# Attention of two tiles done together every second tile in a chunked-attention and SoLU feed-forward kernel

## The chip, the cores and the metric

The kernel runs on one core of a Trainium2 chip. The metric is the device time of one execution in microseconds (us), lower is better; three runs of the kernel before gave a median of 517.52 us. A core has TensorE (PE, matrix products into PSUM), VectorE (DVE), ScalarE (ACT), GpSimd (POOL) and SyncE (SP, which issues DMAs); each works through its own instructions in order and waits on semaphores for the others. DMAs are issued here by SyncE, GpSimd and ScalarE.

## The reference

Attention within chunks of 64 positions, for 8 batches of 8 heads with 576 positions and head size 64; its output, 4608 tokens of 512, goes through a feed-forward layer with the SoLU activation (h times its softmax) and a normalization:

```python
scores = scale * np.matmul(q_c, k_c.transpose(0, 1, 2, 4, 3))
attn = softmax of scores (with the maximum taken off, and 1e-09 added to the sum)
out = np.matmul(attn, v_c)
...
x = out, transposed and reshaped to (B * S, H * D)
h = x @ w_in
e = np.exp(h - h_max)
solu = h * e / (sum(e) + 1e-09)
ln = (solu - mu) / np.sqrt(var + 1e-06) * g_ln
return ln @ w_out
```

All inputs are fp32 (the weights arrive as fp64). The layer has 1024 hidden columns.

## The kernel before

**Tiles.** The 4608 tokens are 36 tiles of 128, two chunks of 64 each; a batch is 4.5 tiles. Tile i passes through attention (scores, softmax, values) and then the feed-forward layer. Every large product is made three times with operands split into a high and a low part (`x_h`, `x_l`, `wi_h`, `wi_l`, and so on).

**TensorE's work for a tile.** `scores(i)`: 32 products of 64 x 64, from `QT` and `KT`. `values(i)`: 32 more, from `V` and the transposed attention weights `AT` (in the profile `attn_t`). Both write the PSUM tile `sx` of two banks, scores in one half and values in the other. `ffn_in(i)`: 24 products of 128 x 512 into `ph` (two banks). `ffn_out`: 24 more into `po`, issued in three thirds by `third()`, for a tile three places behind. PSUM has eight banks: `ph` 2, `sx` 2, `tp` 2 (transposes at the start and end of the kernel), `po` 2.

**The way of the attention weights.** `softmax_a(i)` takes the row maximum of the scores (`s_nmax`) and the difference (`e`) on VectorE and the exponential on ScalarE; `softmax_b(i)` sums (`s_sum`), inverts and multiplies on VectorE. `attn_turn(i)` transposes 32 x 32 blocks into `a_b`; after an odd tile, eight DMAs of 64 KB, four of SyncE and four of GpSimd, put the blocks of two tiles into place in `AT`, of which there is one buffer for an even and an odd tile. `x_high` and `x_low` then split the values for `ffn_in`: `x_h` on ScalarE, `x_l` on VectorE.

**The SoLU.** `solu_a`: row maximum `h_nmax` (VectorE) and the exponential `z` with its sum (ScalarE). `solu_b`: product of `ph` and `z` with its sum (VectorE), `nmean` (VectorE, one column), and the mean taken off (ScalarE). `solu_c`: `ssum` and `eps`, one column each on VectorE. `variance`: squares `sq` with their sum (ScalarE), `u` (VectorE, one column), `r` = u to the power -0.5 (GpSimd, one column). `z_turn(i)` transposes blocks of `z` into `z_b`, and after an odd tile 16 DMAs carry them into `z_t`; `z_split` splits that into `z_h` and `z_l`, the operands of `ffn_out`; `store` scales the result by `r` into `o_sb` and stores it (256 KB, issued by ScalarE).

**Order.** Up to the loop, tiles and the conversion of the weights are interleaved by the list of words `START` (one word is one call: `K:7` is `qk_turn(7)`, `q:14` issues 14 loads, `C` converts weights, `F` is a third of `ffn_out`); there the framework's scheduler may reorder instructions. In the loop, from tile 5 on, `order.on` keeps the instructions of each engine in program order. `load_some(n)` issues n of the 32 loads of a batch of queries and keys on SyncE, 72 KB each; `qk_turn` transposes a tile's queries and keys from them on VectorE. Before, one iteration i does, in this order: `load_v` and `qk_turn` of i+3, `z_turn(i-1)`, `z_split`, loads, `ffn_in(i)`, `scores(i+3)`, `values(i+1)`, `solu_a(i)`, a third, `softmax_a(i+3)`, `x_high(i+1)`, `solu_b(i)`, `softmax_b` and `attn_turn` of i+3, loads, `x_low(i+1)`, `solu_c(i)`, a third, `variance(i)`, a third.

All calls of the loop go through the wrapper at line 42, so most rows of the profile show L42, and instructions are told apart by the names of their tiles.

Of the kernel before, what the change touches and what calls it, by code (L numbers as in the profile page):

```python
# [19 lines left out]
S:1 N:2 C:1 n:3 C:1 C:1 A:1 P:5 P:6 v:1 B:1 V:0 S:2 T:1 M:0 X:0 C:1 A:2 v:2 C:1 P:7 N:3  # L20
B:2 Y:0 C:1 V:1 Q:1 T:2 C:1 n:4 S:3 A:3 v:3 q:8 R:0 V:2 M:1 q:8 X:1 N:4 B:3 S:4 C:1 A:4
q:8 Y:1 M:2 z:0:0 q:8 K:5 X:2 Y:2 T:3 V:3 K:6 C:1 z:0:1 R:1 Q:2 S:5 B:4 T:4 A:5 S:6 v:4
V:4 B:5 T:5 v:5 F F A:6 K:7 C:1 B:6 C:1 R:2 M:3 v:6 Z:2 F z:1:0 X:3 Y:3 S:7 M:4 q:14 R:3
z:1:1 X:4 A:7 B:7 Y:4 V:5 U:6 F U:7 q:14 Z:3 R:4 v:7 F F
"""


# [23 lines left out]
def chunk_attention_then_solu_ffn(  # L51
# [10 lines left out]
    nc = tc.nc  # L62
# [9 lines left out]
    NCC = DM // P  # L72
    NFC = FF // P
    SCALE = 1.0 / float(D) ** 0.5
    LO_DVE = (0, 6, 7, 10, 14)
    LO_TT = (0, 1, 3, 5, 6, 8)
    LO_POOL = (0, 1, 3, 4, 5)
# [13 lines left out]
    small = ctx.enter_context(tc.tile_pool(name="small", bufs=3))  # L91
    ps_h = ctx.enter_context(tc.tile_pool(name="ps_h", bufs=1, space=PSUM))
    ps_a = ctx.enter_context(tc.tile_pool(name="ps_a", bufs=1, space=PSUM))
    ps_t = ctx.enter_context(tc.tile_pool(name="ps_t", bufs=2, space=PSUM))
    ps_o = ctx.enter_context(tc.tile_pool(name="ps_o", bufs=2, space=PSUM))

    order = Order(tc)
# [3 lines left out]
        for e in (nc.tensor, nc.vector, nc.scalar, nc.gpsimd, nc.sync)  # L101
    )

    ident = const.tile([P, P], F32, name="ident")
    make_identity(nc, ident)
    mhalf = const.tile([P, 1], F32, name="mhalf")
    nc.gpsimd.memset(mhalf, -0.5)
    g_sb = const.tile([P, NFC], F32, name="g_sb")
    ident_r = const.tile([P, P], F32R, name="ident_r")
    nc.vector.tensor_copy(out=ident_r, in_=ident)  # L110
# [237 lines left out]
    def turn_natural(i):  # L348
        qk_tiles(i)
        for x in range(2):  # L350
            t = nat[:, i % 2, x]
            pt = ps_t.tile([P, HP, P], F32, name="tp")
# [10 lines left out]


    sx = ps_a.tile([P, 2, 2, HP, CH], F32, name="sx")

    def scores(i):
        for hp in range(HP):
# [14 lines left out]
        MS.memset(ES[x][:, :, CH:], 1e-9)  # L383

    def softmax_a(i):
        sv = sx[:, :, 0].rearrange("p j a k -> p a j k")
# [12 lines left out]
        act.activation(e, e, AF.Exp, scale=SCALE)  # L399
        st[i, "e"] = e  # L400
# [17 lines left out]
    def attn_transpose(i):  # L418

        a = st.pop((i, "e"))  # L420
        pt = ps_t.tile([P, HP, P], F32, name="tp")
        for hp in range(HP):
            pe.transpose(
                pt[:, hp, :],
                a[:, 2 * hp:2 * hp + 2, :].rearrange("p j k -> p (j k)"),
                ident,
            )
        for c in range(2):
            cols = slice(c * CH, (c + 1) * CH)
            to = AT[cols, :, i % 2].rearrange("p g (h j) t -> p j h g t", j=2)  # L430
            for j in range(2):
                act.copy(
                    to[:, j],
                    pt[j * CH:(j + 1) * CH, :, cols].rearrange(
                        "p h (g t) -> p h g t", t=32
                    ),
                )
# [20 lines left out]
                        )  # L458

    def values(i):  # L460
        for hp in range(HP):
            for j in range(2):
                for c in range(2):
                    rows = slice(c * CH, (c + 1) * CH)
                    pe.matmul(
                        sx[j * D:(j + 1) * D, c, 1, hp],
                        V[i][rows, 2 * hp + j, :],
                        AT[rows, :, i % 2, 2 * hp + j, :],
                        start=True,
                        stop=True,  # L470
                    )
        if not order.on:
            x_high(i)
            x_low(i)

    def x_high(i):
        xv = sx[:, :, 1].rearrange("p c a t -> p a c t")
        xh = work.tile([P, NCC, P], F32R, name="x_h")
        xl = work.tile([P, NCC, P], F32R, name="x_l")
        xhv, xlv = (x.rearrange("p a (c t) -> p a c t", t=CH) for x in (xh, xl))  # L480
        act.copy(xhv, xv)
        st[i, "x"] = xh, xl

    def x_low(i):
        xv = sx[:, :, 1].rearrange("p c a t -> p a c t")
# [32 lines left out]
    def solu_b(i):  # L518
        ph = st.pop((i, "h")).rearrange("p n f -> p (n f)")
        z, esum = st.pop((i, "he"))  # L520
        zsum = small.tile([P, 1], F32, name="z_sum")
        dve.scalar_tensor_tensor(
            out=z, in0=ph, scalar=1.0, in1=z, op0=ALU.mult, op1=ALU.mult,
            accum_out=zsum,
        )
        nmean = small.tile([P, 1], F32, name="nmean")
        dve.tensor_scalar(
            out=nmean, in0=zsum, scalar1=-1.0 / FF, scalar2=None, op0=ALU.mult
        )
        if order.on:  # L530
            act.activation(z, z, AF.Identity, bias=nmean)
        else:
            pool.tensor_scalar(
                out=z, in0=z, scalar1=1.0, scalar2=nmean, op0=ALU.mult, op1=ALU.add
            )
        st[i, "z"] = z, esum
        if not order.on:
            solu_c(i)

    def solu_c(i):  # L540
        z, esum = st[i, "z"]

        ssum = small.tile([P, 1], F32, name="ssum")
        dve.tensor_scalar(
            out=ssum, in0=esum, scalar1=1e-9, scalar2=None, op0=ALU.add
        )
        eps = small.tile([P, 1], F32, name="eps")
        dve.scalar_tensor_tensor(
            out=eps, in0=ssum, scalar=1e-6, in1=ssum, op0=ALU.mult, op1=ALU.mult
        )  # L550
        st[i, "z"] = (z, eps)

    def variance(i):
        z, eps = st.pop((i, "z"))
        sq = work.tile([P, FF], mybir.dt.bfloat16, name="sq", bufs=1)
        ssq = small.tile([P, 1], F32, name="ssq")
        act.activation(sq, z, AF.Square, accum_out=ssq)
        u = small.tile([P, 1], F32, name="u")
        dve.scalar_tensor_tensor(
            out=u, in0=ssq, scalar=1.0 / FF, in1=eps, op0=ALU.mult, op1=ALU.add  # L560
        )
# [41 lines left out]
    def z_transpose(i, f):  # L603

        z, _ = st[i, "n"]
        pt = ps_t.tile([P, NFC // 2, P], F32, name="tp")
# [8 lines left out]
    def ffn_out(i, part, parts):  # L615
# [2 lines left out]
        halves = 2 if i == NT - 1 else 1  # L618
        if part == 0:
            st[i, "o"] = [  # L620
                (ps_o, ps_t)[x].tile([P, DM], F32, name=("po", "tp")[x])
                for x in range(halves)
            ]
        ops = []
# [36 lines left out]

    def load_g():
        nc.sync.dma_start(g_sb, g_ln.rearrange("(a p) -> p a", p=P))

    loads = []

# [54 lines left out]
    for i in range(first, NT):  # L721
        order.on = i >= ORD

        if i + 3 < NT and next_batch < B and chunk_of(i + 3, 0)[0] == next_batch - 1:
            load_batch(next_batch)
            next_batch += 1
        if i + 3 < NT:
            load_v(i + 3)
            qk_turn(i + 3)
        if not direct(i - 1):  # L730
            z_turn(i - 1)
        z_split(queue[0][0], slice(0, NFC))
        ahead = i == NT - 1
        load_some(4 if i % 2 == 0 else 6)
        ffn_in(i)

        if i + 3 < NT:
            scores(i + 3)
        if i + 1 < NT:
            values(i + 1)  # L740
        solu_a(i)

        def part():
# [5 lines left out]
        part()  # L749
        if i + 3 < NT:  # L750
            softmax_a(i + 3)
        if i + 1 < NT:
            x_high(i + 1)
        solu_b(i)
        if i + 3 < NT:
            softmax_b(i + 3)
            attn_turn(i + 3)
        load_some(3 if i % 2 == 0 else 5)
        if i + 1 < NT:
            x_low(i + 1)  # L760
        solu_c(i)
        part()
        variance(i)
        part()
# [34 lines left out]
```

## Time and profile before

| | |
|---|---|
| runs | 516.67, 517.52, 517.53 us (median 517.52) |
| profiled execution | 519.47 us, of which the span from first to last instruction is 517.7 us |
| mean granted clock of TensorE | 0.98 |
| busy: TensorE, VectorE, ScalarE, GpSimd | 94%, 79%, 52%, 33% of the span |
| chain that ended last | TensorE 82%, VectorE 8%, DMA 3%, ScalarE 2% |

In the profile's rows, L42 is the line of the kernel, `out<-in` names the tiles written and read, `xN` counts instructions, and a bracket shows how long the engine had been idle and what ended that. A row of TensorE that merges several products shows their first start and last end; the ends are modelled, and so starts are compared. "SPq" and "ACTq" are DMA issues of SyncE and ScalarE. "DMA to landing" is the time from the start of an issue to its arrival, for those whose arrival could be told. A row of stretches gives, after the length, the busy time of PE, PEld (weight loads), DVE, ACT and POOL, and then the granted clock of TensorE, the DMA engines' share and GB/s.

### The profile page before, as it was taken

Reading aid. Unit: us, or ns where it says so; the run is one execution under the profiler, and the core shown is the slowest. Engines: PE = TensorE matmul, PEld = TensorE weight load, DVE = VectorE, ACT = ScalarE, POOL = GpSimd, SP = SyncE. Lnnn points to the kernel's source line nnn. Section 1 sums busy time; section 2 is a strip of 40 time slices with the busy share of each in tenths; the row PEclk is TensorE's granted clock in tenths of the full one; section 3 lists DMA queues with packets and bytes.
Section 4 is the critical chain, followed back from the end, with each engine's and each line's share of the span. In section 5 each row is a group of like instructions: output and inputs, shape, how many; then the busy total and the mean of one; then the engine's idle time right before and its main releaser. Section 6 shows DMA issues by size and latency. Waiting matters only on the chain.

```text
span 517.7 us, 11241 instructions
## 1 busy us (share of the span) xinstructions
PE 485.9 (94%) x4190; PEld 388.7 (75%) x4190; DVE 408.5 (79%) x714; ACT 268.3 (52%) x412; POOL 170.2 (33%) x291
## 2 busy tenths in 40 slices
PE   3779879989999999999999999999899999999997
PEld 2355657768887888888888888888688888887876
DVE  5999976777888888888888888888678888874531
ACT  4858764534444455555555555454355554444452
POOL 4774742540413223131313131413231405043300
PEclk9988979989999999999999999999899999999999
DMA  9996794530777566767576448675747434352211
GB/s 272 347 234 149 127 161 75 126 103 22 170 148 172 133 152 140 169 163 152 145 160 153 108 125 163 158 167 147 141 128 157 120 106 126 80 144 73 79 47 48
DMA packets 204454, 72.33 MB, mean 140 GB/s; under 512 B 188592, under 2 KB 189104, under 8 KB 204016
## 3 DMA queue, kind: packets, MB, share of 16 engines
q1 hardware_dynamic: 192800, 49.58, 43.9%
q0 software_dynamic: 6272, 12.60, 9.4%
q10 hardware_dynamic: 5328, 9.44, 4.9%
q8 instruction: 33, 0.54, 0.4%
q14 instruction: 21, 0.17, 0.1%
HBM read 36.97 MB, written 9.44 MB: 90 GB/s over the span
## 4 chain that ended last, share of the span: by engine, by line
PE 82%; DVE 8%; DMA 3%; ACT 2%; issue 2%; SPq 1%; POOL 0%; ACTq 0%; DVEq 0%
PE po L42 39%; PE ph L42 35%; PE sx L42 7%; DVE w_a L42 4%; DMA attn_t<-a_b 2%; PE tp L42 1%; SPq L42 1%; DMA nat<-in_k_dram 1%; DVE w_p L42 1%; DVE h_nmax L42 1%; ACT z L42 1%; DVE z L42 0%; DMA q_st<-in_q_dram 0%; DVE s_sum L42 0%; ACT o_sb L42 0%
## 5 line engine op out<-in xcount | busy, mean ns | idle before, releaser
L42 PE MATMUL ph<-wi_l,x_h 128*128 128x512 f32 x288 | 114.8, 399 | 8.5 <-ACT w_r L42 3.6
L42 PE MATMUL po<-wo_l,z_h 128*128 128x512 f32 (+1 forms) x288 | 115.9, 402 | 0.3 <-ACT z_h L42 0.3
L42 PE MATMUL ph<-wi_h,x_h 128*128 128x512 f32 x288 | 114.4, 397 | 0.0
L42 PE MATMUL po<-wo_h,z_l 128*128 128x512 f32 (+1 forms) x288 | 112.4, 390 | 0.0
L42 PE MATMUL po<-wo_h,z_h 128*128 128x512 f32 (+1 forms) x288 | 112.3, 390 | 0.0
L42 ACT ACTIVATE z<-ph,h_nmax 128x1024 f32<-128x1024 f32 x36 | 40.2, 1116 | 138.6 <-DVE h_nmax L42 138.6
L42 DVE TENSOR_REDUCE h_nmax<-ph 128x1 f32<-128x1024 f32 x36 | 44.0, 1223 | 48.7 <-PE ph L42 48.6
L42 POOL DMA_DIRECT2D z_t<-z_b x136 | 67.6, 505 | 36.3 <-DVE z_b L42 32.0
L42 PE MATMUL ph<-wi_h,x_l 128*128 128x512 f32 x288 | 78.5, 391 | 0.7 <-DVE x_l L42 0.7
L42 POOL TENSOR_TENSOR r<-u,mhalf 128x1 f32<-128x1 f32 x36 | 20.5, 569 | 175.7 <-DVE u L42 165.1
L42 PEld LDWEIGHTS ph<-wi_l,x_h 128*128 128x128 f32 x288 | 55.3, 192 | 21.5 <-ACT wo_l L42 4.0
L42 PEld LDWEIGHTS po<-wo_l,z_h 128*128 128x128 f32 x288 | 54.5, 189 | 12.8 <-ACT z_h L42 0.7
L42 PEld LDWEIGHTS ph<-wi_h,x_h 128*128 128x128 f32 x288 | 55.3, 192 | 11.5
L42 PEld LDWEIGHTS ph<-wi_h,x_l 128*128 128x128 f32 x288 | 54.3, 189 | 12.8 <-DVE x_l L42 1.4
L42 PEld LDWEIGHTS po<-wo_h,z_l 128*128 128x128 f32 x288 | 54.4, 189 | 11.9 <-DVE z_l L42 0.4
L42 PEld LDWEIGHTS po<-wo_h,z_h 128*128 128x128 f32 x288 | 54.6, 189 | 10.0
L42 POOL DMA_DIRECT2D attn_t<-a_b x60 | 29.5, 498 | 73.3 <-PE po L42 64.3
L42 DVE SCALAR_TENSOR_TENSOR z<-ph,z 128x1024 f32<-128x1024 f32 x36 | 43.9, 1219 | 5.7 <-ACT z L42 5.5
L42 ACT CAST z_h<-z_t 128x1024 fp32r<-128x1024 f32 (+1 forms) x35 | 35.1, 1002 | 23.7 <-DMA attn_t<-a_b 13.5
L42 DVE TENSOR_TENSOR z_l<-z_t,z_h 128x1024 fp32r<-128x1024 f32 (+1 forms) x35 | 39.6, 1132 | 8.7 <-ACT z_h L42 8.7
L42 DVE STREAM_TRANSPOSE z_b<-z 128x1024 f32<-128x1024 f32 x33 | 39.9, 1210 | 2.6 <-POOL z L42 1.3
L42 ACT ACTIVATE z<-z,nmean 128x1024 f32<-128x1024 f32 x31 | 35.7, 1153 | 10.1 <-DVE nmean L42 10.1
(97 smaller groups left out, 676.0 us busy)
## 6 DMA issues: line engine op xcount, KB each, us to landing
out_dram<-o_sb ACTq DMA_DIRECT2D x35, 256.0 KB, 3.1
v_sb<-in_v_dram SPq DMA_DIRECT2D x32, 256.0 KB, 3.7
z_t<-z_b SPq DMA_DIRECT2D x128, 64.0 KB, 2.8
z_t<-z_b POOLq DMA_DIRECT2D x128, 64.0 KB, 2.5
q_st<-in_q_dram SPq DMA_DIRECT2D x112, 72.0 KB, 2.5
k_st<-in_k_dram SPq DMA_DIRECT2D x112, 72.0 KB, 2.5
w_raw<-in_moe_w_out_dram SPq DMA_DIRECT2D x4, 1024.0 KB, 9.6
attn_t<-a_b SPq DMA_DIRECT2D x60, 64.0 KB, 2.3
```

What stands on the lines that cost most here:

```text
L42: ins = make(*args, **kwargs)
```

## The change

The attention products of two tiles are issued together in odd iterations: scores of i+3, values of i+1, scores of i+4, values of i+2. Even tiles keep `sx`; odd tiles use the two banks of `tp`, which become one tile `TP` that `bank()` hands out by halves outside the loop. Queries and keys are turned one tile earlier (`qk_turn(i+4)`), and `START` gets `K:8` and four more loads. In even iterations `x_high` and `x_low` of i+1 stand ahead of `ffn_in(i)`; in odd ones `x_low` stands ahead of `softmax_b`.

In the SoLU, the single-column operations `nmean`, `ssum` and `eps` on VectorE are gone: the product is taken with -1, and the next operation scales it by -1024 with the sum as its bias; 1024 comes back out in the scale of `sq` and in `g_sb`, which is scaled once on GpSimd. `eps` is one Square on ScalarE, and `u` an addition on GpSimd.

```diff
-V:4 B:5 T:5 v:5 F F A:6 K:7 C:1 B:6 C:1 R:2 M:3 v:6 Z:2 F z:1:0 X:3 Y:3 S:7 M:4 q:14 R:3
-z:1:1 X:4 A:7 B:7 Y:4 V:5 U:6 F U:7 q:14 Z:3 R:4 v:7 F F
+V:4 B:5 T:5 v:5 F F A:6 K:7 C:1 B:6 C:1 R:2 M:3 v:6 Z:2 F z:1:0 X:3 Y:3 S:7 K:8 M:4 q:14 R:3
+z:1:1 X:4 A:7 B:7 Y:4 V:5 U:6 F U:7 q:18 Z:3 R:4 v:7 F F
...
-    ps_t = ctx.enter_context(tc.tile_pool(name="ps_t", bufs=2, space=PSUM))
+    ps_t = ctx.enter_context(tc.tile_pool(name="ps_t", bufs=1, space=PSUM))
...
+    TP = ps_t.tile([P, 2, FF // 2], F32, name="tp")
+    banks = 0
+
+    def bank():
+        nonlocal banks
+        banks += 1
+        return TP[:, banks % 2]
...
+    sy = TP.rearrange("p j (s a k) -> p j s a k", s=2, k=CH)
+
+    def attn(i):
+        return sy if order.on and i % 2 else sx
...
             out=z, in0=ph, scalar=-1.0, in1=z, op0=ALU.mult, op1=ALU.mult,
             accum_out=zsum,
         )
-        nmean = small.tile([P, 1], F32, name="nmean")
-        dve.tensor_scalar(
-            out=nmean, in0=zsum, scalar1=-1.0 / FF, scalar2=None, op0=ALU.mult
-        )
         if order.on:
-            act.activation(z, z, AF.Identity, bias=nmean)
+            act.activation(z, z, AF.Identity, scale=-float(FF), bias=zsum)
...
+    def variance(i):
+        z, esum = st.pop((i, "z"))
         eps = small.tile([P, 1], F32, name="eps")
-        dve.scalar_tensor_tensor(
-            out=eps, in0=ssum, scalar=1e-6, in1=ssum, op0=ALU.mult, op1=ALU.mult
-        )
+        act.activation(eps, esum, AF.Square, scale=1e-3, bias=tiny)
...
-        act.activation(sq, z, AF.Square, accum_out=ssq)
+        act.activation(sq, z, AF.Square, scale=1.0 / (FF * 32), accum_out=ssq)
         u = small.tile([P, 1], F32, name="u")
-        dve.scalar_tensor_tensor(
-            out=u, in0=ssq, scalar=1.0 / FF, in1=eps, op0=ALU.mult, op1=ALU.add
-        )
+        pool.tensor_tensor(out=u, in0=ssq, in1=eps, op=ALU.add)
...
         nc.sync.dma_start(g_sb, g_ln.rearrange("(a p) -> p a", p=P))
+        nc.gpsimd.tensor_scalar(
+            out=g_sb, in0=g_sb, scalar1=1.0 / FF, scalar2=0.0, op0=ALU.mult, op1=ALU.add
+        )
...
-        if i + 3 < NT and next_batch < B and chunk_of(i + 3, 0)[0] == next_batch - 1:
+        if i + 4 < NT and next_batch < B and chunk_of(i + 4, 0)[0] == next_batch - 1:
...
         if i + 3 < NT:
             load_v(i + 3)
-            qk_turn(i + 3)
+        if i + 4 < NT:
+            qk_turn(i + 4)
...
+        if i % 2 == 0 and i + 1 < NT:
+            x_high(i + 1)
+            x_low(i + 1)
         load_some(4 if i % 2 == 0 else 6)
         ffn_in(i)
 
-        if i + 3 < NT:
-            scores(i + 3)
-        if i + 1 < NT:
-            values(i + 1)
+        if i % 2 == 1:
+            for m in (i + 1, i + 2):
+                if m + 2 < NT:
+                    scores(m + 2)
+                if m < NT:
+                    values(m)
         solu_a(i)
...
         part()
         if i + 3 < NT:
             softmax_a(i + 3)
-        if i + 1 < NT:
+        if i % 2 == 1 and i + 1 < NT:
             x_high(i + 1)
         solu_b(i)
+        if i % 2 == 1 and i + 1 < NT:
+            x_low(i + 1)
...
         load_some(3 if i % 2 == 0 else 5)
-        if i + 1 < NT:
-            x_low(i + 1)
-        solu_c(i)
         part()
         variance(i)
         part()
```

More of the change, by code (lines that the diff above doesn't have):

```diff
@@ L74, in chunk_attention_then_solu_ffn @@
     SCALE = 1.0 / float(D) ** 0.5
+    assert FF == 32 * 32
     LO_DVE = (0, 6, 7, 10, 14)
@@ L107, in chunk_attention_then_solu_ffn @@
     nc.gpsimd.memset(mhalf, -0.5)
+    tiny = const.tile([P, 1], F32, name="tiny")
+    nc.gpsimd.memset(tiny, 1e-12)
     g_sb = const.tile([P, NFC], F32, name="g_sb")
@@ L351, in turn_natural @@
             t = nat[:, i % 2, x]
-            pt = ps_t.tile([P, HP, P], F32, name="tp")
+            pt = bank().rearrange("p (a t) -> p a t", t=P)
             for hp in range(HP):
@@ L365, in chunk_attention_then_solu_ffn @@
     sx = ps_a.tile([P, 2, 2, HP, CH], F32, name="sx")
+    sy = TP.rearrange("p j (s a k) -> p j s a k", s=2, k=CH)
+    def attn(i):
+        return sy if order.on and i % 2 else sx
     def scores(i):
+        sx = attn(i)
         for hp in range(HP):
@@ L385, in softmax_a @@
     def softmax_a(i):
-        sv = sx[:, :, 0].rearrange("p j a k -> p a j k")
+        sv = attn(i)[:, :, 0].rearrange("p j a k -> p a j k")
         nmax = small.tile([P, HP, 2], F32, name="s_nmax")
@@ L420, in attn_transpose @@
         a = st.pop((i, "e"))
-        pt = ps_t.tile([P, HP, P], F32, name="tp")
+        pt = bank().rearrange("p (a t) -> p a t", t=P)
         for hp in range(HP):
@@ L460, in values @@
     def values(i):
+        sx = attn(i)
         for hp in range(HP):
@@ L476, in x_high @@
     def x_high(i):
-        xv = sx[:, :, 1].rearrange("p c a t -> p a c t")
+        xv = attn(i)[:, :, 1].rearrange("p c a t -> p a c t")
         xh = work.tile([P, NCC, P], F32R, name="x_h")
@@ L484, in x_low @@
     def x_low(i):
-        xv = sx[:, :, 1].rearrange("p c a t -> p a c t")
+        xv = attn(i)[:, :, 1].rearrange("p c a t -> p a c t")
         xhv, xlv = (x.rearrange("p a (c t) -> p a c t", t=CH) for x in st[i, "x"])
@@ L522, in solu_b @@
         dve.scalar_tensor_tensor(
-            out=z, in0=ph, scalar=1.0, in1=z, op0=ALU.mult, op1=ALU.mult,
+            out=z, in0=ph, scalar=-1.0, in1=z, op0=ALU.mult, op1=ALU.mult,
             accum_out=zsum,
         )
-        nmean = small.tile([P, 1], F32, name="nmean")
-        dve.tensor_scalar(
-            out=nmean, in0=zsum, scalar1=-1.0 / FF, scalar2=None, op0=ALU.mult
-        )
         if order.on:
-            act.activation(z, z, AF.Identity, bias=nmean)
+            act.activation(z, z, AF.Identity, scale=-float(FF), bias=zsum)
         else:
             pool.tensor_scalar(
-                out=z, in0=z, scalar1=1.0, scalar2=nmean, op0=ALU.mult, op1=ALU.add
+                out=z, in0=z, scalar1=-float(FF), scalar2=zsum, op0=ALU.mult, op1=ALU.add
             )
         st[i, "z"] = z, esum
-        if not order.on:
-            solu_c(i)
[L540 to L545, printed above, removed]
-        )
-        eps = small.tile([P, 1], F32, name="eps")
-        dve.scalar_tensor_tensor(
-            out=eps, in0=ssum, scalar=1e-6, in1=ssum, op0=ALU.mult, op1=ALU.mult
-        )
-        st[i, "z"] = (z, eps)
-    def variance(i):
-        z, eps = st.pop((i, "z"))
+    def variance(i):
+        z, esum = st.pop((i, "z"))
+        eps = small.tile([P, 1], F32, name="eps")
+        act.activation(eps, esum, AF.Square, scale=1e-3, bias=tiny)
         sq = work.tile([P, FF], mybir.dt.bfloat16, name="sq", bufs=1)
         ssq = small.tile([P, 1], F32, name="ssq")
-        act.activation(sq, z, AF.Square, accum_out=ssq)
+        act.activation(sq, z, AF.Square, scale=1.0 / (FF * 32), accum_out=ssq)
         u = small.tile([P, 1], F32, name="u")
-        dve.scalar_tensor_tensor(
-            out=u, in0=ssq, scalar=1.0 / FF, in1=eps, op0=ALU.mult, op1=ALU.add
-        )
+        pool.tensor_tensor(out=u, in0=ssq, in1=eps, op=ALU.add)
         r = small.tile([P, 1], F32, name="r", bufs=7)
@@ L605, in z_transpose @@
         z, _ = st[i, "n"]
-        pt = ps_t.tile([P, NFC // 2, P], F32, name="tp")
+        pt = bank().rearrange("p (a t) -> p a t", t=P)
         for m in range(NFC // 2):
@@ L620, in ffn_out @@
             st[i, "o"] = [
-                (ps_o, ps_t)[x].tile([P, DM], F32, name=("po", "tp")[x])
+                ps_o.tile([P, DM], F32, name="po") if x == 0 else bank()
                 for x in range(halves)
```

1 line of the change is left out of this document (removed).

## The prediction

> **What bounds the kernel now.** I read the page's engine table first, then the waits of TensorE, the chain of work that ended last, and the timeline of two steady iterations. "Even" and "odd" are the parity of the loop's tile i; T is the start of an iteration's last first-layer product (`ph`).
>
> ```profile
> PE 485.9 (94%) x4190; PEld 388.7 (75%) x4190; DVE 408.5 (79%) x714; ACT 268.3 (52%) x412; POOL 170.2 (33%) x291
> ```
>
> ```profile
> 229.60 1.09 PE sx L42 x64
> 230.69 5.67 PE po L42 x24
> 236.36 5.44 PE ph L42 x24
> ```
>
> ```profile
> PE sx L42 <- DMA attn_t<-a_b: 2.1, 2, 1.8
> ```
>
> The chain's rows (start, length, what) show TensorE alone through the loop: 24 first-layer products, one attention block of 64 small ones, 24 second-layer products (`po`). The last fence is the only row that the waits of TensorE from 130 to 470 us give: it waited twice, both times for the attention weights' transposing copies, `attn_t<-a_b`. So the order of TensorE's products and the landing of those copies decide this change. The timeline has the rest (start, length, engine, operation; idle before in brackets):
>
> ```profile
> 228.53 1.07 PE L42 MATMUL ph<-wi_h,x_l 128*128 128x512 f32 x4
> ...
> 229.53 0.70 PE L42 MATMUL sx<-kT,qT 64*64 64x64 f32 x32
> 229.63 1.23 DVE L42 TENSOR_REDUCE h_nmax<-ph 128x1 f32<-128x1024 f32 x1 [1.50 <-PE ph L42]
> ...
> 230.04 0.65 PE L42 MATMUL sx<-attn_t,v_sb 64*64 64x64 f32 x32
> ...
> 230.62 0.50 PE L42 MATMUL po<-wo_l,z_h 128*128 128x512 f32 x1
> ...
> 232.34 0.39 PE L42 MATMUL po<-wo_h,z_h 128*128 128x512 f32 x1
> ...
> 233.28 0.08 DVE L42 DVE_READ_ACCUMULATOR z<-ph,z 128x1 f32 x1
> 233.40 0.15 DVE L42 TENSOR_SCALAR nmean<-z_sum 128x1 f32<-128x1 f32 x1
> 233.47 0.68 DVE L42 TENSOR_REDUCE s_sum<-e 128x8 f32<-128x520 f32 x1
> ...
> 233.59 1.15 ACT L42 ACTIVATE z<-z,nmean 128x1024 f32<-128x1024 f32 x1 [0.25 <-DVE nmean L42]
> ...
> 234.77 1.06 ACT L42 ACTIVATE sq<-z 128x1024 bf16<-128x1024 f32 x1
> ...
> 235.15 0.71 DVE L42 STREAM_TRANSPOSE a_b<-e 128x512 f32<-128x512 f32 x1
> ...
> 235.74 0.19 ACT L42 ACTIVATION_READ_ACCUMULATOR sq<-z 128x1 f32 x1
> ...
> 235.79 0.65 DVE L42 TENSOR_TENSOR x_l<-sx,x_h 128x512 fp32r<-128x512 f32 x1
> 235.93 2.52 SPq L42 DMA_DIRECT2D attn_t<-a_b  x4
> 235.97 0.39 PE L42 MATMUL po<-wo_h,z_l 128*128 128x512 f32 x1
> ...
> 236.19 0.39 PE L42 MATMUL ph<-wi_l,x_h 128*128 128x512 f32 x1
> ...
> 236.40 1.96 POOL L42 DMA_DIRECT2D attn_t<-a_b  x4 [4.87 <-PE po L42]
> 236.44 0.69 ACT L42 ACTIVATE o_sb<-po,r 128x512 f32<-128x512 f32 x1 [0.52 <-issue]
> ...
> 237.16 0.34 ACTq L650 DMA_DIRECT2D out_dram<-o_sb  x1
> ...
> 239.31 1.18 DVE L42 TENSOR_TENSOR z_l<-z_t,z_h 128x1024 fp32r<-128x1024 f32 x1
> ...
> 242.24 0.84 PE L42 MATMUL sx<-attn_t,v_sb 64*64 64x64 f32 x32
> ```
>
> The reader is to see VectorE run without a gap from `h_nmax` (229.63) to the end of `a_b` (235.86), SyncE issue its four copies 0.07 later, GpSimd its own from 236.40, and TensorE reach the first product that reads them at 242.24, 6.31 after SyncE began.
>
> **The change part by part.**
>
> *Fewer switches between large and small products.* From 232.34 to 235.97 there are 16 steps of 0.227. The last `ph` starts at 228.53 + 3 x 0.227 = 229.21 = T; the first score comes 0.32 later, 0.09 over a step. From the first `po` to the next `ph` it is 5.57 for 24 products, 0.13 over 24 x 0.227 = 5.44. So a visit to attention costs 0.22 beyond its own products, and what the first small products lose is hidden in merged rows: 0 to 0.05. I take 0.25. Before, the loop visits attention in i = 5 to 34, 30 times; after, in odd i from 5 to 33, 15 times. Gain 15 x 0.25 = 3.8 us, all on TensorE's path (ends 3.3 and 4.1). No product is added or removed.
>
> *The copies' deadline moves.* Values of i+1 in an odd iteration need the copies issued in the even iteration before. That even iteration loses its attention block. After: T, then 24 `po` and 24 `ph` with no switch (last start T + 10.88), 0.32 to the first score, 0.51 of scores (229.53 to 230.04), so values at T + 11.71; before at 242.24, T + 13.03. The deadline comes 1.32 earlier. VectorE's chain from `h_nmax` to `a_b` has the same operations except `nmean`, which holds up the next one by about 0.08. So SyncE's first issue stands 5.07 ahead of the values, not 6.31. When did the copies land? The rows of that tile in two windows:
>
> ```profile
> L42 SPq DMA_DIRECT2D attn_t<-a_b x4: 512/564/693, 235.9 to 237.8; - x4
> L42 POOL DMA_DIRECT2D attn_t<-a_b x4: 496/496/498, 236.4 to 237.9; - x4
> ...
> DMA to landing us min/median/max: 1.9/2.9/4.0
> ```
>
> ```profile
> L42 SPq DMA_DIRECT2D attn_t<-a_b x4: 513/564/627, 387.0 to 388.8; - x4
> L42 POOL DMA_DIRECT2D attn_t<-a_b x4: 496/496/496, 387.4 to 388.9; - x4
> DMA to landing us min/median/max: 2.2/3.0/3.6
> ```
>
> The last landings are at most 237.8 + 4.0 = 241.8 and 388.9 + 3.6 = 392.5: 5.9 and 5.5 after SyncE's first issue. Against 5.07 that is a wait of 0.4 to 0.8 per pair if nothing else changes. One thing does: the store of the output, 256 KB, is issued at 237.16, in the middle of the copies. It follows `o_sb`, which will no longer wait for `po` (over 0.7 before `a_b` ends) but for ScalarE: `z` 0.15 earlier (no `nmean`), then a new one-column Square of about 0.2, then `sq`, its read at 235.74, and `o_sb` at once instead of 0.52 later. That puts the store about 0.25 earlier, and I let the copies gain as much: 5.25 to 5.65, a wait of 0.2 to 0.6, taken as 0.4. It blocks TensorE, whose products run in order; behind it stand the rest of the block and `po`, so the whole loop shifts. Even i from 6 to 30: 13 x 0.4 = 5.2 us. In i = 33 no scores stand ahead of the values, so the deadline is 0.5 tighter, before as after, and the kernel before waits there already:
>
> ```profile
> 467.16 0.69 PE L42 MATMUL sx<-attn_t,v_sb 64*64 64x64 f32 x30 [0.29 <-DMA attn_t<-a_b]
> ```
>
> The whole shift of 1.24, less 0.25 for the store, is lost there: 1.0 more. Together +6.2 (ends 0 and 10).
>
> *Tile input split earlier.* For even i, `x_high` and `x_low` of i+1 move ahead of `ffn_in(i)`; VectorE's 0.65 there falls into the 1.50 of idle time before `h_nmax`, in the longer of the two half-periods (odd to even: two blocks of at least 1.09, `po` 5.57, `ph` 5.44, over 13 us). For odd i, `x_low` moves ahead of the softmax sums and puts `a_b` of the first half of a pair 0.65 later; that half has no copies of its own. Cost 0; if VectorE fell behind, `z_l` would be late for `po`. It ends at 240.49; in an even iteration `po` would start 5.44 after 236.19, at 241.63. Over a microsecond is left.
>
> *Single columns.* `nmean`, `ssum`, `eps`, `u` leave VectorE: four operations of about 0.15, on an engine with idle time in each iteration. One Square joins ScalarE (52% busy). `u` goes to GpSimd as a second operation like `r`:
>
> ```profile
> L42 POOL TENSOR_TENSOR r<-u,mhalf 128x1 f32<-128x1 f32 x36 | 20.5, 569 | 175.7 <-DVE u L42 165.1
> ```
>
> 0.57 more in GpSimd's queue, behind the copies in even iterations and ahead of `z_t`'s eight issues after odd ones, with 175.7 us of idle time before `r` to cover it; `r` is used an iteration or more later. Cost 0. At the end of the kernel `nmean` stands on the last tile's chain: gain 0.25.
>
> *Loads.* Queries and keys are turned a tile earlier, so SyncE's loads of a batch begin an iteration earlier, with the same quotas on the other parity: a batch's 32 issues still fit into the four iterations before its first use. Cost 0; the order past the copies in SyncE's queue stays.
>
> *Start.* `K:8` and four more loads move ahead of the loop (two transposes, about 1.4 on VectorE), some 20 single-column operations of 0.15 leave VectorE, and the gains' scaling adds one small GpSimd operation. The stretch is not kept in program order, so it can be laid out anew.
>
> ```profile
> 0.00:113.00 113.00, 86.80 (x746) 62.65 (x747) 94.00 (x171) 69.32 (x128) 61.73 (x76) 0.93 0.75 179
> ```
>
> TensorE idles 26.2 of these 113 us. I take 0, ends -2 and +2.
>
> *Sum.* -3.8 + 6.2 - 0.25 = +2.1 us. The profiled execution took 519.47 us (span 517.7), 1.95 over the median of the three runs. It holds an event that those may lack:
>
> ```profile
> 362.24 1.96 POOL L42 DMA_DIRECT2D attn_t<-a_b  x4 [7.76 <-issue]
> ...
> 367.28 0.88 PE L42 MATMUL sx<-attn_t,v_sb 64*64 64x64 f32 x30 [1.82 <-DMA attn_t<-a_b]
> ```
>
> ```profile
> 364.60:375.00 10.40, 8.58 (x89) 7.06 (x89) 7.69 (x16) 4.61 (x7) 0.72 (x2) 0.84 0.74 140
> ```
>
> GpSimd issued its copies 3.4 late, waiting for nothing the profile shows; TensorE stood still for 1.82 and its granted clock fell to 0.84 over the next 10 us. I keep it in both: 519.47 + 2.1 = 521.6 for an execution like the profiled one, 517.52 + 2.1 = **519.6** against the median.
>
> **Rivals.**
>
> *No wait: the copies land in time.* They'd have to land within 5.07 of SyncE's first issue. For: the `z_t` copies of the same size, with no store among them, take less on GpSimd's queue.
>
> ```profile
> z_t<-z_b POOLq DMA_DIRECT2D x128, 64.0 KB, 2.5
> ```
>
> GpSimd's last issue starts 2.0 after SyncE's first, so 2.0 + 2.5 = 4.5 would do; the loads issued ahead of the copies also get 1.3 us longer to drain. Against: both windows above show 5.5 or more, and the store still falls among the copies. It decides at 0.45 less latency. Time: 517.52 - 3.8 - 0.25 = 513.5. The Trainium skill ("DMA: Bandwidth & Descriptors", Anatomy of one DMA — SWDGE (gpsimd) path) gives 2.0 us plus bytes over 436 GB/s for such a DMA, an estimate of 2.15 us for 64 KB, and by it there would be no wait; the medians of 2.9 and 3.0 in the rows above disagree.
>
> *Waits that slow the clock.* If each stop of TensorE brought a dip like that at 367.28 (0.16 of 10.4 us, 1.7), 14 of them would add 24: 543. Against: it took a stop of 1.82 to do it. The skill's page "TensorE: Matmul & The Clock Gate" (Part 1) wants an idle window of about 3.4 us; here less was enough.
>
> *The rest moves.* The late issue of GpSimd's copies goes away or comes twice (about 1.8 + 1.7 = 3.5 each), or the start is laid out otherwise: 516 or 523.
>
> **Numbers.** Waits of 0.15 to 0.6 a pair have a chance of 0.5 and give 516.2 to 522.3 (faster 0.05, same 0.12, slower 0.33); no wait 0.3; start or issue 0.14 (0.04, 0.03, 0.07); clock 0.03; nothing of the block's order reaching the chip's time 0.03. About 0.2% (1.0 us) is what this kernel's runs can tell from no change. Faster: 0.30 + 0.05 + 0.04 = 0.39; same 0.12 + 0.03 + 0.03 = 0.18; slower 0.33 + 0.07 + 0.03 = 0.43. The range goes from the no-wait end (512.8, all of 4.1 saved and a little at the start) to 522.5.
>
> **What would show it.** Right: 5.44 us from the first `po` to the next `ph` in even iterations; TensorE waits for `attn_t<-a_b` in most odd iterations, tenths of a microsecond each; loop pairs of 24.7 instead of 24.6. Wrong: no such waits and pairs near 24.35 (no wait), `po` waiting for `z_l` (VectorE), or a first loop iteration that starts over 2 us away from before.

## The result and the profile after

The changed kernel takes 533.66 us (530.7 to 536.65) against 517.52 (516.67 to 517.88) before: a ratio of 1.031, interval 1.026 to 1.037. The forecast was 519.6 with a range of 512.8 to 522.5. The place and the kind of wait came as forecast, and so did the sign, for which the chances were close (slower 0.43, faster 0.39). The size did not.

The waits of TensorE from 110 to 480 us, after (engine, line, what was waited for: us in all, times, longest):

```profile
PE sx L42 <- DMA attn_t<-a_b: 16.5, 13, 2.7
PE sx L42 <- DMA k_st<-in_k_dram: 1.0, 1, 1.0
PE po L42 <- DVE z_l L42: 0.7, 2, 0.4
```

Before there were two waits for the copies, 2.1 us. Now there is one in every odd iteration from 7 on. The row for `k_st` is one of them: the products that waited there read `attn_t` and `v_sb`, and the last copy landed 0.24 us before they started. At i = 25 there are two, 4.0 us together; the copies of i = 8 cost 2.7; the others up to i = 31 are 0.55 to 1.45, 1.0 on average, not 0.4. The timeline of one steady pair (even i = 14; T is the last `ph` of that iteration, 236.63) shows why:

```profile
237.06 1.23 DVE L42 TENSOR_REDUCE h_nmax<-ph 128x1 f32<-128x1024 f32 x1 [1.38 <-PE ph L42]
...
240.83 1.15 ACT L42 ACTIVATE z<-z,z_sum 128x1024 f32<-128x1024 f32 x1 [0.55 <-DVE z L42]
...
241.88 0.28 ACT L42 ACTIVATE eps<-h_sum,tiny 128x1 f32<-128x1 f32 x1
...
242.07 1.04 ACT L42 ACTIVATE sq<-z 128x1024 bf16<-128x1024 f32 x1
...
242.40 0.71 DVE L42 STREAM_TRANSPOSE a_b<-e 128x512 f32<-128x512 f32 x1
...
243.11 0.67 ACT L42 ACTIVATE o_sb<-po,r 128x512 f32<-128x512 f32 x1
243.18 2.79 SPq L42 DMA_DIRECT2D attn_t<-a_b  x4
...
243.81 0.35 ACTq L652 DMA_DIRECT2D out_dram<-o_sb  x1
```

```profile
247.83 0.69 PE L42 MATMUL sx<-kT,qT 64*64 64x64 f32 x32
248.35 0.28 PE L42 MATMUL sx<-attn_t,v_sb 64*64 64x64 f32 x2
249.45 0.63 PE L42 MATMUL sx<-attn_t,v_sb 64*64 64x64 f32 x27 [0.83 <-DMA attn_t<-a_b]
```

`a_b` ends at 243.11, 6.48 after T (the prediction had 6.57), and the first values start at 248.35, 5.24 later. From SyncE's first issue it is 5.17 (the prediction had 5.07). So the deadline was right. Two of the values' products start, whose copy is there, and the rest wait. The copies are what is late. Their rows in the window from 236 to 250 us, and the store's in the one from 243.1 to 250 (name, engine, count, size, median from issue to landing):

```profile
L42 SPq DMA_DIRECT2D attn_t<-a_b x4: 512/562/966, 243.2 to 245.0; - x4
...
DMA to landing us min/median/max: 2.0/3.6/4.3
```

```profile
out_dram<-o_sb ACTq DMA_DIRECT2D x1, 256.0 KB, 3.4
```

The median landing was 2.9 before and is 3.6 now. From the figures of the Trainium skill ("DMA: Bandwidth & Descriptors", Anatomy of one DMA — SWDGE (gpsimd) path) the estimate is 2.15 us for 64 KB; the trace is far from it while the store is among the copies.

The profiled execution took 536.65 us, 17.2 more than that of before (519.47). By the starts of TensorE's blocks in the timeline:

| part | before | after | difference | forecast |
|---|---|---|---|---|
| start, up to the first product of tile 7 | 137.75 | 137.81 | +0.1 | 0 ± 2 |
| the 11 steady pairs, mean | 24.59 a pair | 25.38 a pair | +8.7 (11 x 0.79) | +1.7 |
| the pair that waits for the copies of i = 8 | 24.69 | 28.56 | +3.9 | +0.15 |
| the pair that waits for the copies of i = 24 | 28.12 | 30.74 | +2.6 | +0.15 |
| the last pair (tiles 33 and 34) | 24.07 | 24.54 | +0.5 | +0.75 |
| end | 32.61 | 34.03 | +1.4 | -0.25 |

A pair runs from the first product of an odd tile to that of the next odd one; the forecast for a pair is a wait of 0.4 less 0.25 for the visit. The first product of tile 5 comes 1.9 later than before (113.36 against 111.43), but nothing is left of that at tile 7: before, TensorE stood 2.23 us ahead of that product and then took 6.95 us for the tile's 24 products, at a slower clock (0.50 from 111.6 to 115.0), where the changed kernel takes 5.21.

For the copies of i = 8 TensorE stood still for 2.7 us, and its clock went down with it. The chain of waits from 160 to 180 us and the stretch from 160 to 175 (length, busy time of the engines, granted clock, DMA share, GB/s):

```profile
165.71 6.17 DMA attn_t<-a_b
...
172.01 0.95 PE sx L42 x27
```

```profile
160.00:175.00 15.00, 12.31 (x167) 10.33 (x167) 10.44 (x17) 6.50 (x12) 3.71 (x6) 0.90 0.48 104
```

After that stop the starts of the next 28 scores spread over 0.73 us instead of 0.40, and the clock of the stretch is 0.90 (before it was 1.00 in the same stretch). The Trainium skill ("TensorE: Matmul & The Clock Gate", Part 1) asks for an idle window of about 3.4 us; a stop of 2.7 sufficed here, as 1.82 did before. At the end the last half product now goes to a bank that `z_l` has to free:

```profile
525.73 0.38 PE L42 MATMUL tp<-wo_l,z_h 128*128 128x256 f32 x1 [1.28 <-DVE z_l L42]
```

### The profile page after: what moved, and what is told of

The parts are those of the page before. It is cut to its first block, busy times and chain, and to the rows that moved or that the text cites. A ratio compares the mean times of both kernels' runs of the same rounds, so it can differ in the third digit from the quotient of the medians.

```text
span 534.9 us, 11156 instructions
## 1 busy us (share of the span) xinstructions
PE 483.7 (90%) x4190; PEld 389.4 (73%) x4190; DVE 395.8 (74%) x570; ACT 270.2 (51%) x448; POOL 191.6 (36%) x329
## 4 chain that ended last, share of the span: by engine, by line
PE 47%; DVE 26%; DMA 14%; SPq 5%; issue 4%; ACT 3%; POOL 1%; ACTq 0%; POOLq 0%
PE po L42 23%; PE ph L42 18%; DMA attn_t<-a_b 11%; SPq L42 4%; DVE w_a L42 4%; PE tp L42 3%; DVE e L42 3%; DVE h_nmax L42 3%; DVE z L42 3%; PE sx L42 3%; DVE s_sum L42 2%; DVE s_nmax L42 2%; DVE a_b L42 2%; DMA z_t<-z_b 1%; DVE w_p L42 1%
## 5 line engine op out<-in xcount | busy, mean ns | idle before, releaser
L42 PE MATMUL po<-wo_l,z_h 128*128 128x512 f32 (+1 forms) x288 | 114.3, 397 | 0.3 <-ACT z_h L42 0.2
L42 DVE TENSOR_TENSOR z_l<-z_t,z_h 128x1024 fp32r<-128x1024 f32 (+1 forms) x35 | 40.8, 1165 | 41.7 <-ACT z_h L42 41.7
L42 POOL TENSOR_TENSOR u<-ssq,eps 128x1 f32<-128x1 f32 x36 | 8.5, 237 | 139.6 <-ACT sq L42 139.3
L42 ACT ACTIVATE o_sb<-po,r 128x512 f32<-128x512 f32 (+1 forms) x36 | 24.3, 676 | 34.6 <-POOL r L42 18.5
L42 ACT ACTIVATE z<-z,z_sum 128x1024 f32<-128x1024 f32 x31 | 35.7, 1153 | 11.6 <-DVE z L42 11.1
```

The lines of the kernel that those rows point to most:

```text
L42: ins = make(*args, **kwargs)
```

## The experiments

Times are medians; ratios are to the kernel before on the same chip, with their intervals. "Landing" is that of the last of the eight copies, "store" the issue of the even iteration's store; both count from the end of `a_b`. "Deadline" is the start of the first values. Waits are those from 110 to 480 us, with the ones at i = 25.

**One half of the change alone.** First (e1), before with the folded SoLU and nothing else:

```diff
-        nmean, ssum, eps, u on VectorE
+        scale and bias in the activations; eps on ScalarE, u on GpSimd
```

> The kernel before with the single-column edits alone (attention of each tile in its own iteration, as before). If the earlier deadline of the attention weights' copies makes the loss (deadline theory), this part is nearly free: VectorE's chain is 0.17 us shorter, the store 0.6 us earlier, the copies have some 6.4 us as before, TensorE waits little: 515 to 519 us. If the folding makes the loss (u and r queued on GpSimd, a Square on ScalarE, a store that falls earlier among the copies, a start laid out otherwise), this kernel takes it nearly whole: 525 to 534.

524.37 us, ratio 1.011 (1.007 to 1.015). Neither theory had this. The loop runs at before's pace (24.57 to 24.65 a pair) with a single wait for the copies. But the first product of tile 5 comes at 116.98 instead of 111.43, of which 3.9 are left at tile 7 (141.69 against 137.75), and the pair at i = 24 costs 2.3 more. So the folding's cost is in the start, which the framework lays out anew, and at i = 24, not in the steady pairs. The changed kernel has the folding too, and its start costs nothing, so this isn't a price that it pays.

Second (e2), the pairing with the old single-column operations:

```diff
-        folded SoLU
+        nmean, solu_c (ssum, eps), u as before
```

> The changed kernel with the old single-column operations on VectorE: only the pairing of attention is left. Deadline theory: the values stand 5.1 us after the copies' issue, which land after 5.6 to 6.0, so TensorE waits 0.5 to 0.9 us in each of 14 odd iterations and gains 0.25 by each of 15 visits saved: 521 to 527 us. Folding theory: 513 to 517.

524.05 us, ratio 1.012 (1.008 to 1.016). It is 9.6 us faster than the whole change. The waits of TensorE:

```profile
PE sx L42 <- DMA attn_t<-a_b: 5.5, 6, 1.5
PE sx L42 <- issue: 2.6, 2, 2.0
```

Of the second row 2.0 stand at i = 25, behind GpSimd's late issue for i = 24. In most pairs the copies land at 5.0 to 5.3 against a deadline of 5.06. Its store is issued at 0.67, in the full change at 0.70. This became the main question; e13 and e14 below answer it.

**The deadline later or the copies earlier.** Both scores ahead of both values (e3), which puts the deadline 0.47 later:

```diff
-                scores(m + 2); values(m)      (for m = i+1, i+2 in turn)
+                scores(m + 2)                 (for both)
+                values(m)                     (then for both)
```

> The changed kernel with both tiles' scores ahead of both tiles' values in an odd iteration; nothing else is moved. Deadline theory: the first values start 0.47 us later, so each of 13 waits is 0.47 shorter and none is added: 6 to 8 us less than the changed kernel, 525 to 528. If the copies are slow because TensorE's block or the queues hold them (so that the wait follows the block), or the loss lies elsewhere: 532 to 535.

527.91 us, ratio 1.020 (1.015 to 1.024): 5.8 less than the change, as a deadline predicts (13 x 0.47 = 6.1). Landing stays where it was (6.3), the waits fall to 10.7 us.

Then the softmax of even iterations ahead of the SoLU on VectorE (e4):

```diff
+        if i % 2 == 0: softmax_a(i + 3)          (ahead of ffn_in)
...
-        softmax_a(i + 3); x_high; solu_b(i); x_low; softmax_b(i + 3); attn_turn(i + 3)
+        softmax_b(i + 3); attn_turn(i + 3); solu_b(i); x_low      (even i)
```

> The changed kernel, where in even iterations the maximum and difference of the softmax of tile i+3 stand ahead of the first-layer products (its scores are there since the iteration before), its sums and the turn into a_b ahead of the SoLU's product, and x_low behind that. Deadline theory: a_b ends about 2.4 us earlier, the copies land 1 us or more before the values, all waits but that at the late GpSimd issue go: 515 to 519 us. If the loss lies elsewhere: 530 or more; if VectorE becomes late for h_nmax or the SoLU's product for the next first-layer products, between.

512.77 us, ratio 0.990 (0.986 to 0.993), below the 515 that the theory allowed at least. The same pair as above, in the timeline of this kernel:

```profile
231.63 0.71 DVE L42 STREAM_TRANSPOSE a_b<-e 128x512 f32<-128x512 f32 x1
...
232.41 2.42 SPq L42 DMA_DIRECT2D attn_t<-a_b  x4
...
236.49 0.37 ACTq L652 DMA_DIRECT2D out_dram<-o_sb  x1
...
240.09 0.75 PE L42 MATMUL sx<-attn_t,v_sb 64*64 64x64 f32 x29
```

`a_b` ends 7.75 ahead of the values, and the store comes 4.14 after it, when the copies are nearly through. One wait of 1.0 us is left in the loop, and a pair takes 24.19: 0.40 less than before. That is the worth of a saved visit to attention; the prediction took 0.25.

**The store's place.** `eps` moved from ScalarE to GpSimd (e5), to have the store earlier:

```diff
-        act.activation(eps, esum, AF.Square, scale=1e-3, bias=tiny)
+        pool: eroot = esum * 1e-3 + 1e-12; eps = eroot * eroot
```

> The changed kernel with eps on GpSimd (two one-column operations there) instead of a Square on ScalarE, so that o_sb and the output's store come about 0.2 us earlier, at 0.5 us after a_b's end instead of 0.70; a_b, the deadline and the queues are as in the changed kernel. Order theory: what made the copies late is that the store's issue at 0.70 falls just behind SyncE's second copy (issued at 0.68); ahead of it, as in the kernel with the pairing alone (0.67), they land 5.0 to 5.3 after a_b's end instead of 6.0 to 6.7, the waits shrink to 0 to 0.3 and the time to 520 to 524. If the copies are late for another reason of the folding, or the store's nearness alone counts: 531 to 535.

538.54 us, ratio 1.043 (1.037 to 1.049). The experiment missed its aim: the store stayed at 0.72. `sq` starts 1.24 to 1.25 after `z` with or without `eps` between them (241.26 after 240.01, in the changed kernel 242.07 after 240.83), so `eps` on ScalarE costs nothing. Landing and waits are those of the change (6.3; 16.5 us in 13). One burst, that of i = 6, had its store at 0.66, where it landed within 2.27 and not 3.4; its copies still landed at 6.04. The 4.9 us more are not settled; in the profiles (539.00 against 536.65) 1.6 stand ahead of tile 7, and the clock dips once more, after a stop of 1.84 for the copies of i = 22.

Even iterations' stores through SyncE, behind the copies (e6):

```diff
-            nc.scalar.dma_start(out...)
+            sync.dma_start(out...)     (even i)
```

> The changed kernel with the output's store of even iterations issued by SyncE behind the copies and three loads instead of by ScalarE among the copies. If the store among the copies is what delays them: they land 4.6 to 5.2 after a_b's end, the waits go, the loop's pairs take 24.2 us and the time is 516 to 520. If they are late for their own number (eight at once) or for the loads behind them: 530 or more.

526.12 us, ratio 1.019 (1.014 to 1.024). The copies landed at 4.95 in the median, 1.3 earlier than in the change with the same deadline, and the steady pair took 24.20. The rows of the window from 236.4 to 243 us, and the waits of the loop:

```profile
attn_t<-a_b SPq DMA_DIRECT2D x4, 64.0 KB, 2.4
attn_t<-a_b POOLq DMA_DIRECT2D x4, 64.0 KB, 2.5
```

```profile
PE sx L42 <- DMA attn_t<-a_b: 5.7, 5, 2.6
PE po L42 <- ACT z_h L42: 2.3, 1, 2.3
```

So it is the store that makes the copies late. What the time kept above the forecast is SyncE's queue, where one tile's `z_t` copies now came late for `z_h` (2.3 us, with the clock still at 1.00, and 0.5 more for `z_l`), the pair at i = 24 (31.3 us, 7.1 over a steady one), the start and the end.

The store ahead of the squares on ScalarE (e9):

```diff
-        variance(i); part()
+        part(); variance(i)       (even i; the last part issues the store)
```

> The changed kernel; in even iterations ScalarE scales and stores the finished output ahead of the squares, not behind them. Nothing is left out. The store's issue should go from 0.70 us after the end of a_b to about 0.0, ahead of the copies' first issue. Theory 'store's place' (the copies land late because the store's packets come between SyncE's first and second copy): with its packets gone before the second copy's, the last copy lands 4.7 to 5.2 us after a_b, as in the run whose stores stand behind the copies, against a deadline of 5.24: nearly no waits, pairs of 24.2 us, 515 to 521 us. Rival 'bandwidth' (256 KB of store within the same few microseconds, wherever it stands): landing stays at 5.8 to 6.5, 529 to 535 us.

522.39 us, ratio 1.009 (1.006 to 1.011); 'store's place' holds in landing (5.28) and pairs (24.2), and misses the time by 1.4. The waits in the loop are 2.7 us for the copies (1.6 of them at i = 25), 2.4 at i = 25 behind GpSimd's late issue, and 2.4 for `z_h` and `z_l`. The store itself now lands 2.2 us after its issue, not 3.4.

The store 0.67 later, behind a second Square of 512 columns (e10):

```diff
+            act.activation(sq[:, :HALF], z[:, :HALF], AF.Square, ...)
             act.activation(o, po, AF.Copy, scale=r)
```

> The changed kernel; in even iterations ScalarE squares 512 columns once more into a scratch tile ahead of scaling the output, which holds the store back by about 0.6 us. Nothing is left out. The store's issue should be at 1.3 us after a_b, where the kernel before had it, with the changed kernel's deadline of 5.24. This is the case that the prediction's sum was made for. Theory 'store's place': landing at 5.5 to 6.0 as before, waits of 0.25 to 0.75 a pair instead of 0.7 to 1.5, 522 to 528 us. Rival 'bandwidth': landing and time as in the changed kernel, 531 to 536 us. A third one, ScalarE: z_h comes 0.6 later and second-layer products wait for z_l; then TensorE's waits name z_l, and the time is above 530.

532.91 us, ratio 1.028 (1.024 to 1.033): the rival's number. With the store at 1.37 the copies land at 6.10, hardly earlier than with the store at 0.70 (6.27); TensorE waits 14.1 us for them. Within this stretch the store's place makes 0.2 us. So even with the store where the kernel before had it, landing was not the 5.3 to 5.7 that my sum used.

The squares of even iterations over 896 columns, which leaves the other 128 out of the variance, and so a store 0.11 earlier (e13):

```diff
-        act.activation(sq, z, AF.Square, ..., accum_out=ssq)
+        act.activation(sq[:, :896], z[:, :896], AF.Square, ..., accum_out=ssq)   (even i)
```

> The changed kernel; in even iterations the squares and their sum leave out the last 128 of 1024 columns, so that the output's scaling and its store come about 0.13 us earlier: 0.57 after a_b instead of 0.70. Theory 'race' (a store issued up to about 0.67 after a_b gets its packets out within 0.9 us, one issued from 0.70 on waits behind GpSimd's first copy and holds up the last two copies): packets start at 1.5 instead of 2.1, the last copy lands 5.0 to 5.3 after a_b instead of 6.2, against a deadline of 5.24; TensorE's waits for it fall from 16.5 us in all to 2 to 6, and the time to 520 to 526 us. Rival 'folding' (something else in the folded SoLU delays the copies, and the 0.03 us are chance): landing stays near 6.2 and the time at 531 to 535 us.

526.74 us, ratio 1.016 (1.012 to 1.020), 6.9 less than the change. And the pairing alone with a store 0.09 later (e14):

```diff
+            act.activation(idle, z[:, :1], AF.Square)
             act.activation(o, po, AF.Copy, scale=r)
```

> The pairing with the old single-column operations; in even iterations one more operation of a single column, whose result nothing reads, stands on ScalarE ahead of the output's scaling and moves the store from 0.67 to about 0.8 to 0.95 us after a_b. Nothing is left out. Theory 'race': packets start at 2.1 or later and last 1.6, the last copy lands 5.9 to 6.5 after a_b against a deadline of 5.06; TensorE's waits rise from 5.5 us in all to 14 to 18, and the time to 531 to 537 us. Rival 'folding': landing stays at 5.0 to 5.3 and the time at 522 to 526 us.

535.3 us, ratio 1.033 (1.030 to 1.036): 11 us more than the pairing alone, for one column. The waits for the copies in e13 and the landing of one store (238.9 to 245 us):

```profile
PE sx L42 <- DMA attn_t<-a_b: 8.7, 12, 1.9
```

```profile
out_dram<-o_sb ACTq DMA_DIRECT2D x1, 256.0 KB, 2.3
```

The same two rows of e14:

```profile
PE sx L42 <- DMA attn_t<-a_b: 16.3, 14, 1.9
```

```profile
out_dram<-o_sb ACTq DMA_DIRECT2D x1, 256.0 KB, 3.4
```

Each kernel turned towards the other when its store moved by a tenth, so the store's place does it and not the folding alone. But e13 went further than 'folding' allowed and not as far as 'race' said: the store was quick again, and the copies landed at 5.80, not 5.0 to 5.3, with waits of 8.7 us, not 2 to 6. The last data packet of SyncE's four copies ends, in the median, at 4.69 in e2, 4.78 in e13, 5.29 in the change and 5.57 in e14. So in e13 the data are nearly as early as in e2, and what keeps its landing 0.57 later comes after the last packet; whether the folding has a part in that isn't shown. All of it in one table, medians over twelve bursts (i = 6 to 30 without 24):

| kernel | store | store to its landing | copies' landing | deadline | waits, us |
|---|---|---|---|---|---|
| store ahead of squares (e9) | 0.16 (-0.42 to 0.17) | 2.15 | 5.28 | 5.24 | 2.7 |
| squares of 896 columns (e13) | 0.59 | 2.27 | 5.80 | 5.24 | 8.7 |
| pairing alone (e2) | 0.67 | 2.15 | 5.23 | 5.06 | 5.5 |
| the change | 0.70 | 3.43 | 6.27 | 5.24 | 16.5 |
| pairing, one column more (e14) | 0.76 | 3.50 | 6.14 | 5.06 | 16.3 |
| change, store later (e10) | 1.37 | 3.42 | 6.10 | 5.24 | 14.1 |
| stores through SyncE (e6) | 2.6 to 4.9 | 2.53 | 4.95 | 5.24 | 5.7 |
| softmax ahead (e4) | 4.14 | 3.25 | 4.95 | 7.75 | 1.0 |

For the store itself something flips between 0.67 and 0.70: in the median it lands within 2.3 or after 3.4. GpSimd's first copy is issued at 0.54, between SyncE's first and second.

**The rest.** Fewer of GpSimd's issues ahead of i = 24, and the last half product in `sx`, on top of e4 (e7):

```diff
-            (pool if (x + y) % 2 else sync).dma_start(
+            (pool if (x + y) % 2 and not (i == 9 and x >= 2) else sync).dma_start(
...
-                else bank()
+                else sx.rearrange("p j s a k -> p j (s a k)")[:, 1]
```

> The kernel with the early softmax, where four of GpSimd's z_t copies of one pair (i = 10) are issued by SyncE, and the second half of the last tile's output is summed in a bank of sx instead of tp. Count theory of the late GpSimd issue: it is its 129th DMA, so it moves by four issues from the attention weights of i = 24 to the z_t copies of i = 26, where 3 us are to spare: the wait of 1.0 to 1.2 us at i = 24 goes. If it belongs to that time or place, it stays at i = 24. Tail: the wait of 1.3 us for z_l before the last products goes. Together 510 to 512, against 512.8 of the early softmax.

511.46 us, ratio 0.990 (0.987 to 0.993). Both aims were met: the wait at the end is gone, and GpSimd's late issue, its 129th DMA, is now the first of its eight of another transfer, as the count theory said, where nobody waits for it. Its rows in the changed kernel and here:

```profile
372.76 1.97 POOL L42 DMA_DIRECT2D attn_t<-a_b  x4 [9.37 <-issue]
```

```profile
375.90 3.98 POOL L42 DMA_DIRECT2D z_t<-z_b  x8 [5.28 <-DVE s_nmax L42]
```

The other idle times ahead of `z_t` are 2.33, so this one came 2.95 late. The gain over e4 is 1.3 us, within the spread of both.

The pairing with the softmax ahead, without the folding (e8):

```diff
-        folded SoLU
+        nmean, solu_c, u as before          (in e4)
```

> The early softmax and the pairing with the old single-column operations on VectorE. With the copies off the path, the deadline theory has the folding worth nothing in the loop: pairs of 24.2 us as with it, 512 to 514, with the start as the kernel with the pairing alone. If the small operations on VectorE make h_nmax or the next first-layer products late: 515 to 520.

512.49 us, ratio 0.990 (0.988 to 0.993), as e4 with the folding: with the copies off TensorE's path the single columns are worth nothing.

The turning of tile 8 at the end of the start, in e7 (e11):

```diff
-S:7 K:8 M:4 ... v:7 F F
+S:7 M:4 ... v:7 F F K:8
```

> The version with softmax ahead, fewer GpSimd issues and the last half product in a bank of sx; the word K:8 of the start stands at its end instead of in its middle. Nothing is left out. If the turning of tile 8's queries and keys in the middle of the start is what puts the loop's first tile 1.5 to 2.6 us later than in the kernel before (111.43), the first loop product now comes at 111 to 112.5 and the time is 509 to 511 us. Rival: the start is laid out anew by anything that changes in it, and the place of this word decides nothing: first loop product at 113 to 117, 511 to 515 us.

512.12 us, ratio 0.988 (0.983 to 0.993); the first product of tile 5 at 113.81. The rival holds: the place of that word is not what puts the first product of tile 5 later. In the start of both the change and this version the longest wait is the same:

```profile
PE ph L42 <- ACT x_h L42: 4.2, 1, 4.2
```

The store ahead of the squares, with e7's two edits and the late word (e12):

```diff
-        variance(i); part()
+        part(); variance(i)       (even i), and e7's edits without the earlier softmax
```

> The changed kernel with the store ahead of the squares in even iterations, the word K:8 at the end of the start, four of GpSimd's z_t copies moved to SyncE, and the last half product in a bank of sx; softmax stays where it was. Nothing is left out. Theory 'store's place': the place of the store alone does what the earlier softmax did: pairs of 24.2 us, 509 to 513 us. Rival 'slack': landing at 4.7 to 5.2 leaves 0.1 to 0.5 us before the deadline, where the earlier softmax left over 2; bursts that are disturbed then cost waits, 514 to 518 us.

514.85 us, ratio 0.995 (0.992 to 0.998). 'Slack' holds: 1.0 us of waits for the copies and 1.5 for `z_l` are left with steady pairs of 24.2. e4, e7, e8 and e11 (511.5 to 512.8) all beat the kernel before by about 1%, and cannot be told apart.

## Why the prediction was wrong

*What held.* TensorE's order and the copies decide. The deadline came as worked out (5.17 after SyncE's first issue, 5.07 forecast). Even iterations run 5.44 from the first `po` to the next `ph`. VectorE and the new order of the split inputs cost nothing in a steady pair such as the one shown: no wait for them stands in it. In i = 33 the wait is 1.15 against 0.29 before, close to the 1.0 more that was forecast.

*The step that failed* is the one on the store: "That puts the store about 0.25 earlier, and I let the copies gain as much: 5.25 to 5.65, a wait of 0.2 to 0.6, taken as 0.4." The store came 0.60 earlier beside `a_b`. The prediction's own terms make more than its 0.25: 0.15 for `z`, 0.52 for `o_sb`, less 0.2 for the Square and 0.08 for `a_b`, are 0.39. And the 0.2, which no row of before gave, is nothing: `eps` fits into a gap ahead of `sq` (e5). That makes 0.59. But the copies gained nothing; their last landing was 6.27 after `a_b`, 6.2 after SyncE's first issue, 0.75 over the middle of the range. I reasoned that an earlier store frees the copies' way earlier by as much. The runs show no such slope: a store issued anywhere from 0.70 to 1.49 left the landing at 6.1 to 6.3 (change, e14, e10, e1). At 0.16 (e9), at 0.67 without the folding (e2), or behind the copies (e6, e4) it left 4.95 to 5.3; at 0.59 with the folding (e13), 5.80. The price of this step: a steady pair waits about 1.0, not 0.4, and takes 0.79 more than before, not 0.15 (each stop costs some 0.15 more than its row shows); over 11 pairs that is 7.0 of the 15.1 us by which the profiled execution missed, and the stop for the copies of i = 8 is 3.7 more.

Part of that 0.75 lies in the landing that I started from, 5.5 and 5.9 in two bursts. Over the twelve, the kernel before has a median of 5.81 (5.44 to 6.50), yet e10 with the store nearly in before's place has 6.10, and e1 with it at 1.49 has 6.13. In the trace of before, only two to six of the eight arrivals of a burst could be told, so its 5.81 may be too low. GpSimd's last copy is told in all twelve bursts of before, e1 and the change: it lands at 5.64, 5.84 and 6.10. So the copies do come later, by about 0.45 in the change, although its store is earlier; what adds this stays open.

*The switches* were mis-sized the other way: 0.40 a visit instead of 0.25, so 6.0 us and not 3.8. My ends of 3.3 and 4.1 counted only what two rows show; e4 measures the whole.

*Clock.* I gave waits that slow the clock 0.03, with a dip at each of 14 waits. What came was a dip at the stop of 2.7 (copies of i = 8) and at those for i = 24, none at those near 1. The pair at i = 24 costs 2.6 more than before, because GpSimd's late copies now hold up values with an earlier deadline; I had kept that event equal in both. I called these copies 3.4 late; they are 2.9 behind their usual place, which is 0.54 after `a_b`. Why the copies of i = 8 are the latest of all (8.07; 7.78 in e10, 7.19 in e13, 5.75 in e6) is not settled.

*Start and end.* The start came out level, as I took it, but partly by luck: the wait and the slow clock that before had at tile 5 fell elsewhere. In e1 the same folding cost 3.9 there. At the end I forecast -0.25 from `nmean` and missed that `TP` makes the last half product wait 1.28 for `z_l`: +1.4, of which 1.1 is gone in e7.

*Rivals.* "No wait" (513.5, 0.3) asked for a landing within 5.07, and named the store among the copies as what speaks against it. That was the right pivot: e4 and e6 show its steady pairs, at 24.2.

## What to carry to other kernels

When a change moves a deadline, price every transfer that shares the time with the one that is due, by where it stands among its packets, and not by how much earlier it starts. A landing time read in the kernel before need not carry over: here GpSimd's last copy came 0.45 later in the changed one. If copies are near a deadline, move what produces them ahead of work that nobody waits for, here the softmax ahead of the SoLU, instead of tuning the transfers around them: `a_b` then ended 2.5 us earlier, the store fell behind nearly all of the copies, and the single columns were worth nothing (e8).

## What the hardware showed

- One column more on ScalarE moved a 256 KB store's issue from 0.67 to 0.76 us after `a_b` (e2 to e14). The store then took 3.50 us to land and not 2.15, the eight small copies 6.14 and not 5.23, and the time rose by 11 us. Moving it from 0.70 to 0.59 (e13) brought the store back to 2.27, the copies only to 5.80, and the time down by 7 us. The cause inside the queues isn't shown.
- GpSimd's 129th DMA is issued about 3 us late in every profile: before (362.24), in the change (372.76, 14 instructions further on in its queue but the same count of DMAs) and in all versions but three as the first copy of i = 24; in e7, e11 and e12 as part of another transfer. No row names a reason.
- A stop of TensorE near 1 us left its clock alone; 1.82 (before), 1.84 (e5) and 2.7 halved it for 3.4 us, but 1.89 in e14 (i = 31) and 2.33 in e6 (i = 22) did not. The length of a stop alone does not decide it. The slow stretches of a profile last 3.41 us or twice that and lie on one grid of 3.41 us. In the loop at full clock, a slot of that grid with 1.82 us or more of standing still was followed by a slow one in all profiles, and one with up to 1.78 never; the stops of 1.89 and 2.33 each fall across two slots.
